# Idle products on TensorE between attention and the first expert of a mixture of experts

## The chip, the cores and the metric

The kernel runs on one core of a Trainium2 chip. The metric is the device time of one execution in microseconds (us). Engines are named as in the profile: PE (matrix products), DVE (vector), ACT (scalar), POOL (GpSimd) and SP (which issues most of the DMAs).

## The reference, cut to what matters

Linear attention with a feature map, followed by a mixture of experts whose routing picks tokens by their logits in falling order, with a capacity of 576 tokens for each of 8 experts.

```python
def _attn_ref(q, k, v, w_phi):            # (8, 8, 576, 64)
    def phi(x):
        proj = np.einsum('bhsd,df->bhsf', x, w_phi)
        proj = proj - np.max(np.abs(proj), axis=-1, keepdims=True)
        return np.concatenate([np.exp(proj), np.exp(-proj)], axis=-1)
    q_p, k_p = (phi(q), phi(k))
    kv = np.einsum('bhsf,bhsd->bhfd', k_p, v)
    z = np.sum(k_p, axis=2)
    num = np.einsum('bhsf,bhfd->bhsd', q_p, kv)
    den = np.einsum('bhsf,bhf->bhs', q_p, z)[..., None] + 1e-06
    return num / den

def _moe_ref(x, w_gate, w1, w2):          # x (4608, 512), w1 (8, 512, 1024)
    cap = N // E
    flat = (x @ w_gate).flatten()
    for idx in np.argsort(-flat):
        tok, e = idx // E, idx % E
        if assigned[tok] >= 0 or counts[e] >= cap:
            continue
        assigned[tok] = e
        counts[e] += 1
    for e in range(E):
        mask = assigned == e
        out[mask] = np.maximum(x[mask] @ w1[e], 0.0) @ w2[e]
```

## The kernel before

The work comes in three parts, one behind the other on PE.

**Attention** (to about 321 us in the profile) runs over 16 units of two batches and two heads. Each unit transposes its rows (L130), projects them (L158), forms kv and z (L196, L201, L242) and last the numerators (`num`, L285), which DVE divides (L301). The order of all these steps is made by a planner (`Plan`): it holds a list of steps with an engine, a duration and a due time, and steps of PE take one of four PSUM tiles (`D0` to `D3`) as a slot. The last two `num` end PE's part of attention. The gate's logits come out of the same products, and DVE sums them into `L`.

**The routing of the first expert** (`routing(0)` in `moe`, about 321 to 348 us) is not planned. It is written out in order. It does not take tokens one by one: it finds the logit that is the 576th by a search over the digits of the best logit of each token, six digits of 5 or 6 bits. A round works on one digit:

- DVE compares all tokens with all values of the digit (`cmp`, L520; for the first digit L472), in several chunks;
- PE counts for each value and expert how many tokens reach it: 36 products, one for each 128 tokens, whose weights are the comparisons, 32 or 64 columns wide, and which stream the 8 columns of the experts (L530). The first digit was counted in part during attention; only 9 products are left for it (L473);
- DVE turns the counts into flags (`fl`, L545 or L546);
- PE sums the flags over the digit's values by one product with ones (L548, the flag product);
- DVE takes the largest sum (L550) and moves the tokens' keys by it (L554).

After the sixth round DVE knows the expert (`ei`, L568; SP reads it and starts the loads of `w1`) and the tokens that belong to it. Two products (L582, L583) add up how many such tokens stand ahead of each row, the offsets. DVE and POOL then build two one-hot matrices (`lo` at L606, `hv` at L600), 18 products (L611) turn them into the list of tokens, and four more (L618) lay it out as the index `idx`.

Tiles of this part that PE writes lie in PSUM: `rps` with two buffers, and `h0` to `h3` and `y0`, `y1`, with one buffer each. With one buffer, a new tile under the same name may be written only when all that used the last one is done.

**The feed-forward** runs over the eight experts, again in a planner's order; the later experts' routing is spread among it. Ahead of it stands a loop of 36 products of ones with ones, of 128 columns each, whose results nobody reads (L831 to L833; `warm` is 36). Then, for the first expert, POOL gathers the tokens' rows by indirect DMA (L738), PE transposes them (L743), ACT and DVE split them (L744, L745), and the products with `w1` (L767) and `w2` (L796) follow. For each product three are run, with high and low parts. All the other experts' products follow on the same queue.

At the head of the kernel seven products of a tile of zeros (`w`, named `warm`) with 512 columns each are issued in the same manner (L102 to L104).

Of the kernel before, what the change touches and what calls it, by code (L numbers as in the profile page):

```python
# [7 lines left out]
F32 = mybir.dt.float32  # L8
# [82 lines left out]
def attention(ctx, tc, nc, q, k, v, w_phi, w_gate, xs, L, C, xp, cfg={}, after=None, later=None, count=None, init=iter(())):  # L91

    B,H,S,D=q.shape
# [4 lines left out]
    ps=ctx.enter_context(tc.tile_pool(name='aps',bufs=1,space=PS))  # L98
    ident=C['ident']
    V,A,G,PE=nc.vector,nc.scalar,nc.gpsimd,nc.tensor  # L100

    w=sb.tile([128,512],BF,name='warm',bufs=1); V.memset(w,0.0)  # L102
    p=ps.tile([128,2,512],F32,name='D0',bufs=1)
# [20 lines left out]
    P=Plan(d['stay']*1e3); P.swc,P.swA,P.swO,P.wp=90.,85.,35.,d['wp']  # L124
    ND_=4
# [193 lines left out]
    for i in range(40):  # L319
        def some(x,n=1 if i<39 else 99):  # L320
            for _ in range(n):
                if next(init,0): break
        P.add(('init',i),'DVE',300.,d['init']+i*d['pitch'],some,[('init',i-1)] if i else [],lat=95.,after=1e3*(d['init']+i*d['pitch']))
    out=P.order()
    if cfg.get('show'): 
        for x in out: print(round(x['start']),round(x['end']),x['eng'],x['mode'],x['name'])
# [155 lines left out]
def moe(ctx, tc, nc, L, xs, w1, w2, out, C, MC, R0, cfg={}):  # L482
# [3 lines left out]
    V,G,A,PE=nc.vector,nc.gpsimd,nc.scalar,nc.tensor  # L486
    rp=ctx.enter_context(tc.tile_pool(name='rt',bufs=1))
    fp=ctx.enter_context(tc.tile_pool(name='ffn',bufs=2))
    ps=ctx.enter_context(tc.tile_pool(name='fps',bufs=1,space=PS))
# [6 lines left out]
    T={}  # L496
    S=lambda shape,name,dt=F32,b=1: rp.tile(shape,dt,name=name,bufs=b)
    def rps(shape): return ps.tile(shape,F32,name='rps',bufs=cfg.get('rps',2))
    WC=tuple(cfg.get('wc',(1,2,3,3)))
    def routing(r):  # L500

# [2 lines left out]
        if not last:  # L504
            R=R0 if r==0 else state()
            if r: yield from prep(R,0,NT)
            dg,OH=R['dg'],R['OH']
            c=dg[:,0]; lat=cfg.get('lat0',1.2)
            for i,(sh,bits) in enumerate(DIG):
                K=KW[i]; n=128//K; fin=i==ND-1  # L510
                part='n0' in R and i==0
                if part:
                    p=rps([K,8])
                    count0(R,p,NT//9-1)
                else:
                    cmp=S([128,NT//n,K,n],f'cmp{K}',BF,b=2)
                    cv=c.rearrange('p (g i) -> p g i',i=n)
                    g=0
                    for ck in (WC if wide else (9,))*(1 if K==32 else 2):
                        V.tensor_tensor(cmp[:,g:g+ck],cv[:,g:g+ck,None,:].to_broadcast([128,ck,K,n]),  # L520
                                        kt[i].rearrange('p (k i) -> p k i',i=n)[:,None].to_broadcast([128,ck,K,n]),op=OP.is_ge); g+=ck
                if 'rest' in R and i:
                    with tc.issue_after(R['last']):
                        for _ in R.pop('rest'): pass
                yield
                if part: pass
                elif wide:
                    p=rps([K,8])
                    for t in range(NT):
                        PE.matmul(p,cmp[:,t//n,:,t%n],OH[:,t,:],start=t==0,stop=t==NT-1)  # L530
                else:
                    p=rps([128,n,8])
                    for g in range(NT//n):
                        PE.matmul(p,cmp[:,g].rearrange('p k i -> p (k i)'),OH[:,g*n:g*n+n,:],start=g==0,stop=g==NT//n-1)  # L534
                    yield
                    mm=S([128,n,8],f'mm{n}'); V.tensor_mul(mm,p,msk[n])
                    dd=S([128,8,1],'dd',F32R)
                    with nc.allow_low_precision(reason='whole numbers under 2**13'): V.tensor_reduce(dd,mm.rearrange('p i e -> p e i'),axis=AX.X,op=OP.add)
                    yield

                    p=rps([128,8]); PE.matmul(p,Q[n],dd[:,:,0],start=True,stop=True)  # L541
                    yield
                KR=K if wide else 128
                fl=S([KR,8],f'fl{KR}',BF)
                if part: V.scalar_tensor_tensor(fl,p,-float(cap),R['n0'],op0=OP.add,op1=OP.is_ge)  # L545
                else: V.tensor_scalar(fl,p,float(cap),2.0**(-7*i),op0=OP.is_ge,op1=OP.mult)  # L546
                yield
                p=rps([128,8]); PE.matmul(p,ones[0:KR],fl,start=True,stop=True)  # L548
                if r: yield
                ch=S([128,1],'ch'); V.tensor_reduce(ch,p,axis=AX.X,op=OP.max)  # L550
                lat=cfg.get('latd',.7)
                if fin: break
                c2=S([128,NT],'cc',BF,b=2)
                V.scalar_tensor_tensor(c2,c,ch,dg[:,i+1],op0=OP.subtract,op1=OP.add); c=c2  # L554
                if r: yield

            f8=S([128,8],'f8')
            V.scalar_tensor_tensor(f8,p,ch,e8,op0=OP.is_equal,op1=OP.mult)
            c1=S([128,1],'c1'); V.tensor_scalar(c1,ch,-2.0**(-7*(ND-1)),None,op0=OP.add)
            mx=S([128,1],'mx'); V.tensor_reduce(mx,f8,axis=AX.X,op=OP.max)  # L560
        else:
            f8=S([128,8],'f8'); V.tensor_mul(f8,opn,e8)
            mx=S([128,1],'mx'); V.tensor_reduce(mx,f8,axis=AX.X,op=OP.max)
# [17 lines left out]
        p=rps([128,2])  # L581
        PE.matmul(p,tri,tot,start=True,stop=False)  # L582
        PE.matmul(p[:,1:2],low,tot[:,0:1],start=False,stop=True)  # L583
        if r: yield
        off=S([128,2],'off'); V.tensor_copy(off,p)
        rk=S([128,2,NT],'rk')
        for i in range(2):
# [21 lines left out]
        p=rps([128,9,2,2])  # L609
# [4 lines left out]
        if wide:  # L614

            pb=S([128,9,2,2],'pb',BF); V.tensor_copy(pb,p)
            p=rps([128,9])
# [4 lines left out]
        else:  # L622
# [6 lines left out]
            p=rps([128,9,2])  # L629
# [20 lines left out]
    ctx.enter_context(tc.manual_schedule())  # L650

    it0=routing(0)
    for x in it0:
        if x=='ei':
# [12 lines left out]
    P=Plan(d['stay']*1e3); P.SEM=d['sem']; P.wp=d['wp']  # L667
# [21 lines left out]
    for r in range(1,E):  # L689
        it=routing(r)  # L690
        z=steps(r==E-1)
        t=d['TE']*(r-1)+(d['ch'] if r>1 else d['c1'])
        ni=len(z)-(2 if r<E-1 else 1)
        for i,x in enumerate(z):
            def f(y,it=it): next(it,None)
            nm=('idx',r) if i==ni else ('up',r) if i>ni else ('rt',r,i)
            if len(x)>2 and x[2]=='ei':

                nm=('ei',r)
            sl=(('idx',3,('idx',r)),) if i==ni else ()  # L700
            add(nm,x[0],float(x[1]),t+i*d['cp' if r>1 else 'cp1'],f,(prev,),mode=x[2] if x[0]=='PE' else None,slot=sl,lock=x[0]=='DVE')
            prev=nm
# [136 lines left out]
@with_exitstack  # L839
def tile_kernel(ctx, tc, q, k, v, w_phi, moe_w_gate, moe_w1, moe_w2, out):  # L840
    nc = tc.nc
    dp = ctx.enter_context(tc.tile_pool(name='dram', bufs=1, space=bass.MemoryType.DRAM))
    xs = dp.tile([4608, 512], F32, name='xs')
    lp = ctx.enter_context(tc.tile_pool(name='lp', bufs=1))
    L = lp.tile([128, 36, 8], F32, name='L')
    C = consts(ctx, tc, nc, w_phi)
    xp = ctx.enter_context(tc.tile_pool(name='xp', bufs=2))
    rp = ctx.enter_context(tc.tile_pool(name='mc', bufs=1))
    MC, R0 = [], {}

    def init():
        yield from moe_consts(rp, nc, C, L, MC, {'lat0': 2.95, 'latr': 2.33, 'latc': 1.56, 'slack': 0.66, 'slack1': -0.2, 'pre': 0, 'warm': 36, 'wide': 1, 'latd': 0.46, 'lq': 0.96, 'lo': 0.49, 'lm': 1.69, 'lat7': 3.76, 'lgh': 1.56, 'lgx': 1.29, 'xs': 13, 'xb': 3, 'c0': 1, 'x0': 7, 'w0v': 1, 'xn': 4, 'w2o': 22, 'hc': 272, 'r1d': 1.56, 'w2s': 10, 'r1s': 0.0})
        R0.update(MC[0]())

    def prep(bp):
        yield from MC[1](R0, 9 * bp, 9 * bp + 9)

    def after():
        it = prep(3)
        for _ in range(6):  # L860
            next(it)
        R0['rest'] = it

    with ExitStack() as actx:
        attention(actx, tc, nc, q, k, v, w_phi, moe_w_gate, xs, L, C, xp, ATT, after, prep, lambda bp, p: MC[2][1](R0, p, bp), init())
    moe(ctx, tc, nc, L, xs, moe_w1, moe_w2, out, C, MC, R0, {'lat0': 2.95, 'latr': 2.33, 'latc': 1.56, 'slack': 0.66, 'slack1': -0.2, 'pre': 0, 'warm': 36, 'wide': 1, 'latd': 0.46, 'lq': 0.96, 'lo': 0.49, 'lm': 1.69, 'lat7': 3.76, 'lgh': 1.56, 'lgx': 1.29, 'xs': 13, 'xb': 3, 'c0': 1, 'x0': 7, 'w0v': 1, 'xn': 4, 'w2o': 22, 'hc': 272, 'r1d': 1.56, 'w2s': 10, 'r1s': 0.0})
# [27 lines left out]
```

## Time and profile before

| | |
|---|---|
| runs | 821.05, 822.28, 822.49 us (median 822.28) |
| the profiled execution | 824.51 us |
| its span, first to last instruction | 822.7 us |
| mean granted PE clock | 0.968 |
| PE busy | 775.6 us (94%), 9932 products |
| DVE busy | 561.9 us (68%) |
| ACT, POOL busy | 363.1 us (44%), 262.3 us (32%) |

The page gives busy times of each engine, the span in 40 slices, the DMA queues, the chain that ended last and the costliest groups. The timeline lists instructions with their start and length and, in brackets, the idle time before them with what ended it. The busy time by windows gives, for stretches that the reader chooses, the length, then for PE, PE's weight loads, DVE, ACT and POOL the busy time and the count, then the granted PE clock as a share of full speed, the DMA engines' busy share and their GB/s. Times count from the span's start. A product's length in the timeline includes its way through the array, so that products overlap.

### The profile page before, as it was taken

What the parts mean: (1) busy time and instruction counts of PE and PEld (TensorE: products, weight loads), DVE (VectorE), ACT (ScalarE), POOL (GpSimd) and SP (SyncE); (2) the same over time, 40 slices, a digit from 0 to 9 for tenths busy, and PEclk for the clock granted to TensorE, in tenths of its full rate; (3) what the DMA queues carried; (4) which work ended last, traced back from release to release, by engine and by line L of the source; (5) the groups of instructions that cost most, each with busy time, mean ns of one, the idle gap of its engine ahead of it and who ended that gap; (6) DMA issues with size and microseconds to landing.
All of it is one profiled execution on the core that took longest, in us unless ns stands there. A gap on an engine that the chain in (4) does not pass through costs nothing.

```text
span 822.7 us, 23414 instructions
## 1 busy us (share of the span) xinstructions
PE 775.6 (94%) x9932; PEld 671.2 (82%) x9932; DVE 561.9 (68%) x1494; ACT 363.1 (44%) x625; POOL 262.3 (32%) x300
## 2 busy tenths in 40 slices
PE   6889999998999897589999999999999999999995
PEld 5778878887888786579889898798798898897983
DVE  4897897889788775788587577577586686460410
ACT  3656666776666562134342333243243234341410
POOL 2866655555566451120310411302203103402011
PEclk7999999999999899589999999999999999999998
DMA  9744454544554112231633333325315315700300
GB/s 193 159 118 119 120 144 114 149 120 117 149 144 118 31 32 60 88 108 69 199 122 98 102 123 118 96 108 162 110 50 180 141 50 163 269 1 39 122 26 32
DMA packets 73528, 91.79 MB, mean 112 GB/s; under 512 B 5280, under 2 KB 56512, under 8 KB 73424
## 3 DMA queue, kind: packets, MB, share of 16 engines
q1 hardware_dynamic: 67328, 71.32, 29.4%
q0 software_dynamic: 6096, 18.98, 6.7%
q8 instruction: 78, 1.28, 0.7%
q14 instruction: 26, 0.21, 0.1%
HBM read 71.40 MB, written 18.87 MB: 110 GB/s over the span
## 4 chain that ended last, share of the span: by engine, by line
PE 43%; issue 16%; POOL 2%; DMA 0%; POOLq 0%; ACT 0%; ACTq 0%
PE h L767 20%; PE y L796 17%; PE y L811 2%; PE h L743 2%; PE rps L534 1%; POOL out_dram L825 1%; POOL xg L738 1%; DMA xg<-xs,idx 0%; PE rps L611 0%; POOLq L889 0%; PE rps L541 0%; POOL spacer L824 0%; PE rps L548 0%; ACT ysb L819 0%; ACT xh L744 0%
## 5 line engine op out<-in xcount | busy, mean ns | idle before, releaser
L767 PE MATMUL h<-xh,w1h 128*128 128x272 f32 (+1 forms) x512 | 145.7, 305 | 0.7 <-ACT xh L744 0.7
L767 PE MATMUL h<-xh,w1l 128*128 128x304 f32 (+1 forms) x512 | 143.7, 300 | 0.0
L778 ACT ACTIVATE fh<-h 128x272 fp32r<-128x272 f32 (+1 forms) x128 | 49.3, 385 | 134.4 <-PE h L767 116.5
L825 POOL DMA_INDIRECT out_dram<-ysb,idx x40 | 40.7, 1016 | 206.5 <-ACT ysb L819 203.1
L796 PE MATMUL y<-w2h,fl 128*128 128x512 f32 x256 | 102.0, 398 | 0.0
L796 PE MATMUL y<-w2l,fh 128*128 128x512 f32 x256 | 101.9, 398 | 0.0
L796 PE MATMUL y<-w2h,fh 128*128 128x512 f32 x256 | 101.4, 396 | 0.0
L767 PEld LDWEIGHTS h<-xh,w1h 128*128 128x128 f32 x512 | 97.1, 190 | 2.5 <-issue 1.2
L767 PEld LDWEIGHTS h<-xh,w1l 128*128 128x128 f32 x512 | 97.2, 190 | 0.0
L738 POOL DMA_INDIRECT xg<-xs,idx x40 | 39.9, 997 | 178.5 <-issue 141.8
L767 PE MATMUL h<-xl,w1h 128*128 128x272 f32 (+1 forms) x512 | 91.6, 298 | 0.0
L782 DVE SCALAR_TENSOR_TENSOR fl<-h,fh 128x272 fp32r<-128x272 f32 (+1 forms) x128 | 52.9, 420 | 55.3 <-ACT fh L778 34.9
L268 ACT ACTIVATE qP<-D 128x768 f32<-128x768 f32 x96 | 72.4, 809 | 39.9 <-PE D L130 39.9
L209 POOL TENSOR_TENSOR ks<-ks,kP 128x512 f32<-128x512 f32 x64 | 81.9, 1280 | 4.7
L285 PE MATMUL D<-kz,qP 128*64 128x73 f32 x2304 | 80.3, 228 | 2.6 <-DVE kt L165 2.6
L208 POOL TENSOR_TENSOR ks<-kP 128x512 f32<-128x512 f32 x32 | 40.8, 1274 | 124.8 <-issue 96.3
L285 PEld LDWEIGHTS D<-kz,qP 128*64 128x64 f32 x2304 | 75.6, 136 | 5.2 <-DVE kt L165 2.7
L767 PEld LDWEIGHTS h<-xl,w1h 128*128 128x128 f32 x512 | 75.5, 188 | 0.0
L819 ACT COPY ysb<-y 128x512 f32<-128x512 f32 (+1 forms) x40 | 21.8, 545 | 103.7 <-PE y L796 65.7
L162 DVE TENSOR_REDUCE km<-D 128x6 f32<-128x768 f32 x48 | 45.8, 954 | 28.8 <-PE D L158 28.7
L196 PE MATMUL D<-kP,vi 128*64 128x256 f32 x512 | 61.6, 382 | 0.0
L796 PEld LDWEIGHTS y<-w2h,fh 128*128 128x128 f32 x256 | 48.2, 188 | 9.0
(176 smaller groups left out, 1495.0 us busy)
## 6 DMA issues: line engine op xcount, KB each, us to landing
raww<-in_moe_w_dram SPq DMA_DIRECT2D x64, 512.0 KB, 4.9
qi<-in_q_dram SPq DMA_DIRECT2D x32, 288.0 KB, 5.5
xs<-xp SPq DMA_DIRECT2D x16, 576.0 KB, 4.0
ki<-in_k_dram SPq DMA_DIRECT2D x32, 160.0 KB, 3.8
vi<-in_v_dram SPq DMA_DIRECT2D x32, 160.0 KB, 3.1
ki<-in_k_dram SPq DMA_DIRECT2D x32, 128.0 KB, 3.5
vi<-in_v_dram SPq DMA_DIRECT2D x32, 128.0 KB, 3.4
xg<-xs,idx POOLq DMA_INDIRECT x40
```

Source lines behind the costliest of these rows:

```text
L162: V.tensor_reduce(m[:,:,0:n],X['v'],axis=AX.X,op=OP.max,apply_absolute_value=True)
L196: PE.matmul(kv[64*c:64*c+64,i,0:256],v_[:,a,s_,:],kP[:,b,:],start=b in (0,5,9,14),stop=False,skip_group_check=True)
L208: if i==0: G.tensor_add(ks[:,:,a],X(0),X(1))
L209: elif i<3: G.tensor_add(ks[:,:,a],ks[:,:,a],X(i+1))
L268: for fh in range(2): A.activation(rows(qP[:,fh]),halves(X['T'],6),AF.Exp,scale=1.0-2*fh)
L285: PE.matmul(p[64*ab:64*ab+64,c,m:m+73],T['qP',u,jj][:,fh,o,64*ab:64*ab+64],T['kz',u][:,ab,fh,a^ab,:],start=fh==0,stop=fh==1,skip_group_che ...
L738: G.indirect_dma_start(out=T['xg',r][0:n,bb,:],out_offset=None,in_=xs,in_offset=bass.IndirectOffsetOnAxis(ap=T['idx',r][0:n,bb,:],axis=0))
L767: PE.matmul(p,ws[:,k,o:o+128],xx[:,k,o1:o2],start=n==0,stop=n==11)
L778: A.activation(hh[:,f,o1:o1+m1],p[:,0:m1],AF.Relu)
L782: V.scalar_tensor_tensor(hl[:,f,o1:o1+m1],p[:,0:m1],0.0,hh[:,f,o1:o1+m1],op0=OP.max,op1=OP.subtract)
L796: PE.matmul(p,hx[:,f,o:o+128],ws[:,f%2,:],start=n==0,stop=n==23)
L825: st=G.indirect_dma_start(out=ov,out_offset=bass.IndirectOffsetOnAxis(ap=iv,axis=0),in_=yv,in_offset=None)
```

## The change

Three loops of products are added whose results nobody reads.

- `keep`, a step of the planner in attention, behind the last `num`: 14 products of the tile of zeros with 512 columns, into one of the four `D` tiles. The planner puts it behind the last product of attention, ahead of the first count of the routing.
- `idle(9)` behind the flag product of each of the first five rounds, and `idle(24)` behind that of the sixth: products of ones with ones, 128 columns each.
- `idle(36)` behind the two products of the offsets.

`idle` opens a new tile named `h3` for every eight products. `r` is the expert; only the first one's routing (r = 0) gets them. DVE, ACT, POOL and SP have the same instructions in the same order as before. Line numbers behind the first added loop grow by 4, those behind the second by 8, and further on by 9 and 10.

```diff
@@ attention, behind the last unit
+    def keep(x):
+        p=bank(('D','keep'))(x)
+        for _ in range(14): PE.matmul(p[:,0],w[:,0:128],w,start=True,stop=True)
+    P.add('keep','PE',3000.,1e6,keep,[(('num',1),NU-1)],mode='A',slot=(('D',ND_,('D','keep')),),frees=(('D','keep'),))
     out=P.order()
@@ moe
     def rps(shape): return ps.tile(shape,F32,name='rps',bufs=cfg.get('rps',2))
+    def idle(n):
+        for i in range(n):
+            if i%8==0: p=ps.tile([128,512],F32,name='h3',bufs=1)
+            PE.matmul(p[:,0:128],ones,ones,start=True,stop=True)
@@ routing, each round
                 p=rps([128,8]); PE.matmul(p,ones[0:KR],fl,start=True,stop=True)
                 if r: yield
+                else: idle(24 if fin else 9)
                 ch=S([128,1],'ch'); V.tensor_reduce(ch,p,axis=AX.X,op=OP.max)
@@ routing, the offsets
         PE.matmul(p[:,1:2],low,tot[:,0:1],start=False,stop=True)
         if r: yield
+        else: idle(36)
         off=S([128,2],'off'); V.tensor_copy(off,p)
```

PE's order at the end of the sixth round before (`tri` and `low` are the triangular weights of the offsets, `cmp` is here the one-hot matrix `lo`):

```order
L548 LDWEIGHTS onesb
L548 MATMUL rps<-fl_6115,onesb 128x8 [waits DVE_49]
L582 LDWEIGHTS tri
L582 MATMUL rps<-tot,tri 128x2 [waits DVE_49]
L583 LDWEIGHTS low
L583 MATMUL rps<-tot,low 128x1
L611 LDWEIGHTS cmp_6174 [waits DVE_49]
L611 MATMUL rps<-hv,cmp_6174 128x36 [waits Pool_49]
```

With the change, where `idle(24)` ends and `idle(36)` begins (L506 is the product in `idle`):

```order
L506 LDWEIGHTS onesb
L506 MATMUL h_6207<-onesb 128x128
L591 LDWEIGHTS tri
L591 MATMUL rps<-tot,tri 128x2 [waits DVE_49]
L592 LDWEIGHTS low
L592 MATMUL rps<-tot,low 128x1
L506 LDWEIGHTS onesb
L506 MATMUL h_6255<-onesb 128x128 [waits PE_49]
```

The offsets' products now stand behind 24 idle ones, and the index's products behind 36 more; the first product on each new `h3` waits for PE's own earlier ones.

## The prediction

> **What bounds the kernel now.** I read the page's slices first: the busy share of PE and the clock that it was granted.
>
> ```profile
> PE   6889999998999897589999999999999999999995
> PEclk7999999999999899589999999999999999999998
> ```
>
> A slice is 20.57 us. Apart from the start PE is full except in the sixteenth to eighteenth slice (309 to 370 us), where the clock falls to 0.5 and 0.8 as well: the routing of the first expert, between attention and the feed-forward. What comes after it I read from the busy time by windows:
>
> ```profile
> 360.20:815.00 454.80, 453.14 (x3347) 395.80 (x3345) 276.42 (x833) 154.27 (x328) 78.59 (x114) 1.00 0.32 109
> ```
>
> PE (first pair of columns) works 453.14 of these 454.80 us at full clock. So whatever moves the start of the first expert moves the end by as much. The stretch itself, from PE's timeline (start, length, operation; in brackets the idle time before it and who ended it):
>
> ```profile
> 315.94 4.79 PE L285 MATMUL D<-kz,qP 128*64 128x73 f32 x144
> 324.50 0.70 PE L473 MATMUL rps<-OH,cmp 128*32 128x8 bf16 x9 [3.77 <-DVE xp L301]
> 325.60 0.16 PE L548 MATMUL rps<-fl,onesb 32*128 32x8 bf16 x1 [0.40 <-DVE fl L545]
> 326.57 1.43 PE L530 MATMUL rps<-OH,cmp 128*32 128x8 bf16 x36 [0.81 <-DVE cmp L520]
> 328.24 0.16 PE L548 MATMUL rps<-fl,onesb 32*128 32x8 bf16 x1 [0.24 <-DVE fl L546]
> 329.21 1.43 PE L530 MATMUL rps<-OH,cmp 128*32 128x8 bf16 x36 [0.81 <-DVE cmp L520]
> ...
> 334.51 2.24 PE L530 MATMUL rps<-OH,cmp 128*64 128x8 bf16 x36 [0.81 <-DVE cmp L520]
> ...
> 340.44 0.16 PE L548 MATMUL rps<-fl,onesb 64*128 64x8 bf16 x1 [0.25 <-DVE fl L546]
> 342.61 0.16 PE L582 MATMUL rps<-tot,tri 128*128 128x2 bf16 x1 [2.00 <-DVE tot L579]
> 342.63 0.17 PE L583 MATMUL rps<-tot,low 128*128 128x1 bf16 x1
> 346.06 1.25 PE L611 MATMUL rps<-hv,cmp 128*128 128x36 bf16 x18 [3.26 <-POOL hv L600]
> 347.60 0.25 PE L618 MATMUL rps<-pb,dup 128*128 128x9 bf16 x4 [0.29 <-DVE pb L616]
> 347.70 3.24 PE L833 MATMUL h<-onesb 128*128 128x128 bf16 x36
> 352.85 0.63 PE L743 MATMUL h<-ident,xg 128*128 128x128 f32 x4 [1.91 <-DMA xg<-xs,idx]
> 353.97 1.09 PE L743 MATMUL h<-ident,xg 128*128 128x128 f32 x4 [0.49 <-DMA xg<-xs,idx]
> 355.22 1.09 PE L743 MATMUL h<-ident,xg 128*128 128x128 f32 x4 [0.17 <-DMA xg<-xs,idx]
> 356.98 0.59 PE L767 MATMUL h<-xh,w1h 128*128 128x272 f32 x1 [0.67 <-ACT xh L744]
> ```
>
> It is one chain: DVE compares, PE counts (L473, L530), DVE makes a flag, PE sums it (L548), six times over; then the offsets (L582, L583), the index (L611, L618), the gather, the transposes (L743) and the first real product (L767). PE waits in the gaps that the change fills.
>
> **When the clock falls and rises.** Windows of 1 us place the steps (the number behind the last bracket is the granted clock):
>
> ```profile
> 326.00:327.00 1.00, 0.43 (x11) 0.43 (x12) 0.96 (x5) 0.00 (x0) 0.00 (x0) 0.54 1.15 349
> 349.00:350.00 1.00, 1.00 (x13) 1.00 (x11) 0.96 (x4) 0.24 (x1) 0.69 (x2) 0.52 1.06 372
> 353.00:354.00 1.00, 0.51 (x5) 0.30 (x4) 0.00 (x0) 0.48 (x2) 0.77 (x1) 0.69 0.74 172
> 360.00:361.00 1.00, 1.00 (x16) 0.91 (x15) 1.00 (x3) 0.00 (x0) 0.00 (x0) 0.90 0.00 0
> ```
>
> A mean of 0.54 between 1.0 and 0.5 means a fall at 326.08; likewise a rise at 349.96, a fall at 353.38, a rise at 360.20. The distances are 23.88, 3.42 and 6.82 us: seven, one and two times 3.41. So the clock is decided every 3.41 us, from what PE did in between. What counts there? Six such windows:
>
> ```profile
> 268.05:271.46 3.41, 1.70 (x28) 1.18 (x26) 3.41 (x10) 1.06 (x2) 2.08 (x3) 1.00 0.00 0
> 278.29:281.70 3.41, 3.18 (x75) 2.95 (x71) 1.48 (x9) 2.50 (x4) 1.50 (x2) 1.00 0.02 5
> 319.25:322.66 3.41, 1.48 (x48) 1.33 (x42) 3.20 (x17) 0.00 (x0) 0.00 (x0) 1.00 0.03 7
> ...
> 329.49:332.91 3.42, 2.37 (x63) 2.22 (x63) 1.95 (x9) 0.00 (x0) 0.00 (x0) 0.50 0.00 0
> ...
> 346.56:349.97 3.41, 3.02 (x38) 2.82 (x39) 2.47 (x12) 2.09 (x2) 1.16 (x2) 0.50 0.97 330
> 349.97:353.38 3.41, 1.50 (x21) 1.22 (x18) 1.99 (x7) 1.04 (x1) 2.80 (x3) 1.00 0.76 224
> ```
>
> After the first two and the last one the clock falls, after 319.25 it stays, after 346.56 it rises, after 329.49 it stays low although PE looks busy for 2.37 us. Busy time does not decide it (3.18 us fell, 1.48 us stayed). The columns that are streamed do. First their price. L833's 36 products of 128 columns ran 2.26 us at half clock, then, but for a tail of some 0.17, 0.81 us at full: (2.26/2 + 0.81)/36 = 0.054 us each at full clock, 0.107 at half. By columns the window at 319.25, 1.48 us of L285 less the tail, streams 1.3 us, **38%**, and holds. The one at 349.97 has 0.81 us of L833 and four L743 of about (0.63 - 0.17)/4 = 0.115 us: 1.27 us at most, **37%** (less if transposes count less), and falls. The L530 windows stream 8 columns a product, a few per cent, and never rise. The rise came with 22 x 0.107 = 2.35 us of L833 and about 0.3 of L611, **78%**.
>
> **The change part by part.** All of it is PE's work, and nothing else is moved on PE or on any other engine.
>
> *keep*: 14 products of 512 columns, 14 x 4 x 0.054 = 3.0 us, from 320.73 to 323.8. The gap before L473 lasts to 324.50: hidden. It fills the window to 322.66, and the next has 1.1 us of it and 0.45 of the first idle(9): 45%, so that on this grid the fall moves from 326.08 to 329.49.
>
> *What a high clock is worth in a round*: at the low one 36 loads and products take 1.43 us (L530). L473, at clock 1.00, takes 0.70 for nine, no less per product, so the gain is bounded by nothing below and by half of 1.43 above; and DVE sets a floor:
>
> ```profile
> 328.04 0.15 DVE L546 TENSOR_SCALAR fl<-rps 32x8 bf16<-32x8 f32 x1 [0.25 <-PE rps L530]
> ...
> 328.94 0.97 DVE L520 TENSOR_TENSOR cmp<-cc,kt 128x128 bf16<-128x128 bf16 x4
> ...
> 334.23 1.84 DVE L520 TENSOR_TENSOR cmp<-cc,kt 128x128 bf16<-128x128 bf16 x8
> ```
>
> The last of four compares ends at 329.91, and 12 products at half price follow: PE would end at 330.3 instead of 330.64. So 0 to 0.3 us a round; likewise 0 to 0.3 with 64 columns. One more round at full clock: I take **-0.1**.
>
> *idle(9)*: at full clock 9 x 0.054 = 0.49 us in a gap of 0.81. But the ninth product opens a new buffer of the one-buffer tile h3 and waits for the eighth. No row shows a PE product waiting for its direct predecessor; the bounds are nothing, and a product's tail (0.16 for an 8-column product, 0.21 at half clock by the two steps above) plus a wake of 0.05 (L546 ends at 328.19, L548 starts at 328.24): 0.26. I take 0.26. Still hidden at full clock. At half clock: 9 x 0.107 + 0.26 = 1.22 us against 0.97 from L548 to L530 (328.24 to 329.21): L530 is 0.25 late. Three rounds pay this. The first tiles of a round wait for DVE's short compares anyway, which swallows half: **+0.4** (0 to +0.75).
>
> *Does idle(9) hold the clock?* A round lasts 2.64 us (328.24 to 330.88): 0.49/2.64 = 18%; two bursts in one window make 0.97/3.41 = 28%. Both are under the 37% after which it fell.
>
> The Trainium skill's page "TensorE: Matmul & The Clock Gate" ("Why this matters for your kernels") says otherwise: the clock stays up as long as PE has no gap over about 3 us between bursts, and with idle(9) no gap is that long. This trace does not bear that out: the window at 278.29 was 3.18 us busy out of 3.41 and the clock fell.
>
> *idle(24)*: at half clock 24 x 0.107 + 2 x 0.26 = 3.09 us, against 2.17 from L548 to L582: **+0.9** (+0.4 if the waits cost nothing, 0 if the clock is up).
>
> *idle(36)*: at half clock 36 x 0.107 + 4 x 0.26 = 4.9 us against 3.43 from L583 to L611. L611's 18 products also wait for DVE inside, 1.25 us for some 0.55 of work, which gives 0.7 back. And with both blocks PE streams about 77% of the time, as in the window that rose, so the clock should come up on the way (on this grid at 346.56); the rest then costs half. **+0.1** (0 to +0.8).
>
> *L833* ends a microsecond later or earlier; behind it lies the gather's 1.91 us of waiting: nothing.
>
> *The clock at the first expert.* L767 ran 3.2 us at half clock before the rise at 360.20. If it starts 1.3 us later on the same grid, the window to 360.20 is only half full, and the rise waits for 363.6: 5.3 us at half, (5.3 - 3.2)/2 = +1.05. On another grid it is as much the other way. I take **+0.2** (-1.0 to +1.1).
>
> Here is the same on the pieces of PE's order. Round two before (fl is the flag, cmp the comparisons of the next round):
>
> ```order
> L530 MATMUL rps<-OH,cmp_5915 32x8
> L548 LDWEIGHTS onesb
> L548 MATMUL rps<-fl_5957,onesb 128x8 [waits DVE_49]
> L530 LDWEIGHTS cmp_5965 [waits DVE_49]
> L530 MATMUL rps<-OH,cmp_5965 32x8
> ```
>
> With the change, the end of idle(9) in the same round (L506 is idle's product, L538 the old L530):
>
> ```order
> L506 LDWEIGHTS onesb
> L506 MATMUL h_5998<-onesb 128x128
> L506 LDWEIGHTS onesb
> L506 MATMUL h_6007<-onesb 128x128 [waits PE_49]
> L538 LDWEIGHTS cmp_6013 [waits DVE_49]
> L538 MATMUL rps<-OH,cmp_6013 32x8
> ```
>
> The load of cmp now stands behind a product that waits for PE itself. DVE, which waits only for the flag product, isn't touched.
>
> **Sum:** -0.1 + 0.4 + 0.9 + 0.1 + 0.2 = **+1.5 us**. Against the profiled execution that is 822.7 + 1.5 = 824.2 us of span (824.5 + 1.5 = 826.0 with what lies around it). The median of the three runs, 822.28, is 2.2 us below that execution's time; the difference carries over: **823.8 us**.
>
> **The rivals.**
>
> *The clock holds throughout* (idle(9) suffices). For it: only two of the falls lie close to the limit, and what counts is my inference. Then all idle blocks are hidden (24 x 0.054 + 2 x 0.22 = 1.74 against 2.17; 36 x 0.054 + 4 x 0.22 = 2.8 against 3.43), five rounds gain 0 to 0.3, L611 nothing, and half of it is lost again as L767 starts earlier at half clock: -0.3 to -2.5, about -1.2: 821.1 us. This is where the skill's rule leads. Chance 18%.
>
> *The waits on PE itself cost nothing* while the clock falls: idle(9) ends where L530 starts (0.96 against 0.97), idle(24) costs 0.4, idle(36) 0.4 less L611's slack: +0.4: 822.7 us. 20%.
>
> *The clock comes up late* (the slower side): at 77% the window may just miss what it needs; L582's wait in between takes some of it. Then idle(36) runs at half clock to its end and pushes L611 by 0.8 more, and L767 begins 2 us later, with its own late rise: +1.5 + 0.8 + 0.6 = +2.9: 825.2 us. It decides as soon as the share needed is over some 75%. 12%.
>
> *The forecast* (clock falls one window later, waits cost, a rise by idle(36)): 50%.
>
> **How the numbers follow.** Runs of this kernel can be told apart by about 0.2%, 1.64 us (the three before lie 1.4 us apart). The forecast is just inside; with the clock's grid moving it by a microsecond either way, 45% of it is slower by more. Slower: 0.5 x 0.45 + 0.12 x 0.9 + 0.02 = 0.35. Faster: 0.18 x 0.4 + some from the others, 0.07 = 0.14. The rest, 0.51, is within 0.2%. The range takes in the holding clock's middle and the late rise: 820.8 to 825.6.
>
> **What would show it.** Right: the granted clock at 1.0 to about 329.5 and at 0.5 by the fourth round; L538 some 0.1 to 0.25 us late in the rounds at 0.5; the first product of the offsets 2.9 to 3.2 us behind the last flag product; the index products 1 to 1.5 us later than 347.60. Wrong: a clock of 1.0 from 320 to 346; no gap before the ninth idle product; the offsets still 2.17 us behind the last flag product.

## The result and the profile after

The changed kernel is slower: median 826.87 us (826.03 to 828.79, 6 runs) against 822.44 us (821.05 to 824.23, 6 runs), ratio 1.0056 with an interval of 1.004 to 1.0072. Two repetitions (below) gave the changed kernel the same median, 826.76 and 826.86 us, but the kernel before 824.64 and 824.63 us over 34 and 35 runs: ratios 1.0025 (1.001 to 1.0041) and 1.0018 (1.0001 to 1.0034). So the change costs some 2 us (2.1 and 2.2 by the medians, 2.1 and 1.5 by the ratios). The six runs of before in the first measurement were low by about as much, and why stays open. One execution of before at 1499 us and one of e6 at 967 us belong to a far slower state and stand in no median here.

The slices of the changed kernel's page, PE's busy share and its granted clock:

```profile
PE   6899999998999899979999999999999999999995
PEclk9999999999999899589999999999999999999998
```

The page of before had PE at 7, 5 and 8 tenths in the sixteenth to eighteenth slice; now it has 9, 9 and 7. PE is busier and the clock in the seventeenth slice is again 0.5. Windows of 1 us of the changed kernel (granted clock third from the end) place its steps:

```profile
329.00:330.00 1.00, 0.94 (x20) 0.69 (x19) 0.96 (x4) 0.00 (x0) 0.00 (x0) 0.84 0.00 0
...
346.00:347.00 1.00, 0.94 (x11) 0.78 (x9) 0.93 (x4) 0.00 (x0) 0.21 (x1) 0.63 1.09 344
356.00:357.00 1.00, 0.51 (x5) 0.30 (x4) 0.47 (x3) 0.58 (x2) 1.00 (x1) 0.99 0.70 148
363.00:364.00 1.00, 1.00 (x7) 0.88 (x8) 0.97 (x4) 0.37 (x1) 0.00 (x0) 0.59 0.00 0
```

A fall at 329.68 (before 326.08), a rise at 346.75, a fall at 356.99, a rise at 363.81. PE's timeline of the changed kernel (L326 is keep, L506 idle, L538 the count, L556 the flag product, L591 and L592 the offsets, L621 and L628 the index, L777 the first real product):

```profile
320.75 3.20 PE L326 MATMUL D<-warm 128*128 128x512 bf16 x13
324.60 0.70 PE L477 MATMUL rps<-OH,cmp 128*32 128x8 bf16 x9 [0.65 <-DVE xp L301]
...
326.67 1.43 PE L538 MATMUL rps<-OH,cmp 128*32 128x8 bf16 x36
...
330.99 0.16 PE L556 MATMUL rps<-fl,onesb 32*128 32x8 bf16 x1 [0.24 <-DVE fl L554]
331.08 1.35 PE L506 MATMUL h<-onesb 128*128 128x128 bf16 x9
332.36 1.36 PE L538 MATMUL rps<-OH,cmp 128*32 128x8 bf16 x36
333.97 0.16 PE L556 MATMUL rps<-fl,onesb 32*128 32x8 bf16 x1 [0.24 <-DVE fl L554]
...
341.39 0.16 PE L556 MATMUL rps<-fl,onesb 64*128 64x8 bf16 x1 [0.25 <-DVE fl L554]
341.48 3.17 PE L506 MATMUL h<-onesb 128*128 128x128 bf16 x24
344.45 0.21 PE L591 MATMUL rps<-tot,tri 128*128 128x2 bf16 x1
344.52 0.16 PE L592 MATMUL rps<-tot,low 128*128 128x1 bf16 x1
344.71 3.84 PE L506 MATMUL h<-onesb 128*128 128x128 bf16 x36
348.39 0.77 PE L621 MATMUL rps<-hv,cmp 128*128 128x36 bf16 x18
349.44 0.25 PE L628 MATMUL rps<-pb,dup 128*128 128x9 bf16 x4 [0.29 <-DVE pb L626]
```

Attention ends 0.09 us later than in the first profile. Against that, the flag products of the first three rounds stand where they stood; the fourth comes 0.33 us later, the fifth 0.59, the sixth 0.85, the offsets 1.76, the index (349.44 against 347.60) 1.76. The idle time before L538 is gone, and with it the slack.

To compare kernels whose attention ends at different times, I cut each span at the start of the last num, of the last flag product, of the index product and of the first L767. All are starts in PE's timeline, in us:

| profile | to last num | to sixth flag | to index | to first L767 | to the end | last num to end |
|---|---|---|---|---|---|---|
| before | 320.50 | 19.94 | 7.15 | 9.39 | 465.73 | 402.2 |
| before, again (c1) | 320.76 | 19.93 | 7.15 | 9.82 | 466.17 | 403.1 |
| changed | 320.59 | 20.79 | 8.06 | 9.31 | 466.31 | 404.5 |
| changed, again (a1) | 320.10 | 21.13 | 8.06 | 9.32 | 466.36 | 404.9 |
| changed, third (a2) | 320.27 | 20.79 | 8.06 | 9.25 | 466.10 | 404.2 |
| keep alone (e1) | 318.26 | 19.94 | 7.15 | 9.10 | 467.86 | 404.0 |
| no waits (e2) | 318.55 | 20.29 | 7.63 | 9.16 | 465.97 | 403.1 |
| idle(9) alone (e3) | 321.18 | 21.46 | 7.14 | 9.43 | 468.06 | 406.1 |
| the last two blocks (e4) | 319.68 | 19.93 | 8.06 | 9.19 | 466.34 | 403.5 |

From the last num to the end the three profiles with the change average 404.5, the two before 402.65: 1.9 us, close to the repeated timings. Attention's own stretch, the same work in all nine, lies between 318.3 and 321.2 (321.6 in e6 and 317.3 in e9 below). That spread is larger than the effect.

### The profile page after: what moved, and what is told of

The parts are those of the page before. It is cut to its first block, busy times and chain, and to the rows that moved or that the text cites. A ratio compares the mean times of both kernels' runs of the same rounds, so it can differ in the third digit from the quotient of the medians.

```text
span 825.1 us, 23651 instructions
## 1 busy us (share of the span) xinstructions
PE 789.1 (96%) x10050; PEld 679.9 (82%) x10051; DVE 562.1 (68%) x1494; ACT 363.1 (44%) x625; POOL 262.4 (32%) x300
## 4 chain that ended last, share of the span: by engine, by line
PE 45%; issue 12%; POOL 2%; DMA 0%; DVE 0%; POOLq 0%; ACT 0%; DVEq 0%; ACTq 0%
PE h L777 20%; PE y L806 16%; PE y L821 2%; PE h L753 2%; PE rps L542 1%; POOL out_dram L835 1%; PE h L506 1%; PE rps L538 1%; POOL xg L748 1%; DMA xg<-xs,idx 0%; PE rps L621 0%; PE rps L556 0%; POOLq L899 0%; PE rps L549 0%; POOL spacer L834 0%
## 5 line engine op out<-in xcount | busy, mean ns | idle before, releaser
L777 PE MATMUL h<-xh,w1h 128*128 128x272 f32 (+1 forms) x512 | 146.1, 305 | 0.7 <-ACT xh L754 0.7
L777 PE MATMUL h<-xh,w1l 128*128 128x304 f32 (+1 forms) x512 | 143.9, 301 | 0.0
L777 PEld LDWEIGHTS h<-xh,w1h 128*128 128x128 f32 x512 | 97.3, 190 | 2.5 <-issue 1.2
L777 PEld LDWEIGHTS h<-xh,w1l 128*128 128x128 f32 x512 | 97.5, 190 | 0.0
L777 PE MATMUL h<-xl,w1h 128*128 128x272 f32 (+1 forms) x512 | 91.4, 298 | 0.0
L777 PEld LDWEIGHTS h<-xl,w1h 128*128 128x128 f32 x512 | 75.5, 188 | 0.0
```

Source lines behind the costliest of these rows:

```text
L777: PE.matmul(p,ws[:,k,o:o+128],xx[:,k,o1:o2],start=n==0,stop=n==11)
```

## The experiments

The diffs are cut to the changed lines and, where needed, one line beside them.

**c1: the kernel before, once more** (no edit).

> The kernel before, unchanged, once more, for a second profile and for the spread of its runs. In the two profiles the index products (L618) start 1.84 us later with the change and the last product ends 2.35 us later, yet the medians lie 4.4 us apart. Theory A (delay plus a later rise of the clock; the rest is the spread of executions, in which the first profile of before was a slow one): this profile has the same stretch to within 0.2 us (last L285 to L618: 26.9 us), some 2 to 5 us of L767 at half clock depending on where the clock's steps fall, and a span between 819 and 823 us. Theory B (the kernel before usually has the clock up when L767 starts, and the first profile was an exception): under 1 us of L767 at half clock and a span near 820.6 us.

824.61 us, ratio to before 1.0002 (0.9989 to 1.0016). The stretches are those of the first profile to within 0.5 us, with L767 at half clock for 3.0 us. Theory A, but for the span: 823.8 us where 819 to 823 were expected, and the first profile of before, at 822.7 us, was the shorter of the two, so that this part of the theory failed. The 35 runs of before beside it ran from 821.48 to 826.99.

**a1 and a2: the full change, again and a third time** (no edit).

> The full change once more. In the four profiles so far a span is the sum of three stretches: attention to its last num (318.3 to 320.8 us, other from run to run by where the clock falls in it, in kernels whose attention is the same), from there to the first L767 (36.5 and 36.9 us before, 38.2 with the change), and from there to the end (465.7 to 467.9). Theory A (the change's own cost is the middle stretch, +1.3 to +1.7 us, and a later rise of the clock, 0 to +1; the 4.4 us of the first measurement hold 2 us of the executions' spread): 1.3 to 3 us over the kernel before, whose median is now 824.24 over 35 runs: 825.5 to 827.2. Theory B (the cost really is 4.4 us): over 828.

> The full change a third time, since the first measurement gave +4.4 us (6 runs of each) and the second +2.1 (12 and 34 runs). In the profiles, from the last num to the end, it took 404.5 and 404.9 us, the kernel before 402.2 and 403.1. Theory A (its own cost is about 2 us; the rest of the first measurement was the spread of executions): +1.2 to +3.0 us. Theory B (4.4 us is real): +3.5 or more.

+2.1 and +2.2 us by the medians. Theory A both times. In a1 the clock fell at 326.2, a step earlier than in the first profile of the change, so that one round more ran its block at half clock: the sixth flag product comes 1.19 us later instead of 0.85. Where the step falls differs from execution to execution.

**e1: keep alone.**

```diff
-                else: idle(24 if fin else 9)
-        else: idle(36)
```

> Only the 14 products behind the last num are left; the three kinds of idle are taken out. Theory A: they lie in PE's gap, the clock falls one step of 3.41 us later, L530 takes 1.43 us at full clock too, so nothing is gained or lost: within 0.7 us of before (822.4). Rival (the later fall is worth something, or the block itself does harm later on): more than 1 us away from before.

825.23 us, ratio 1.0009 (0.9991 to 1.0027). The time by itself cannot tell; the stretches can: sixth flag product and index are as before to 0.01 us, so keep costs and wins nothing there. The odd number is the last one, 467.86 us, taken up under e5.

**e2: no waits inside a block.**

```diff
-            if i%8==0: p=ps.tile([128,512],F32,name='h3',bufs=1)
+            if i==0: p=ps.tile([128,512],F32,name='h3',bufs=1)
```

> The whole change, but each idle block writes one tile instead of a new h3 for every eight products, so that no product in a block waits for its predecessor. Theory A (the waits on PE itself are a large part): rounds at half clock 0 to 0.1 us late instead of 0.3 each, the offsets 0.4 to 0.6 us behind instead of 0.9, L618 starts 0.5 us late instead of 1.74, and the time is 1 to 2 us under that of the full change: 825 to 826 us. Rival (the cost is in the products at half clock, not in the waits): within 0.7 us of the full change (826.9).

825.23 us, ratio 1.0010 (0.9992 to 1.0028). The index comes 0.83 us late, more than the 0.5 expected. Four of e2's rounds ran at half clock, and so a1 is the one to compare with, which also had four: there the index comes 2.10 us late. The waits are 1.3 us of that, some 60%, and the products at half clock the rest. A round of e2 at half clock, from PE's timeline:

```profile
329.07 0.16 PE L556 MATMUL rps<-fl,onesb 32*128 32x8 bf16 x1 [0.24 <-DVE fl L554]
329.17 1.14 PE L506 MATMUL h<-onesb 128*128 128x128 bf16 x9
330.24 1.35 PE L538 MATMUL rps<-OH,cmp 128*32 128x8 bf16 x36
```

From flag product to count 1.17 us, where before had 0.97 and the full change has 1.37.

**e3: idle(9) alone.** The planner's step keep is taken out too.

```diff
-                else: idle(24 if fin else 9)
+                elif not fin: idle(9)
-        else: idle(36)
```

> Only idle(9) behind the first five flag products is left. Theory A: without the first block the clock falls a step earlier, so that four of the five rounds run it at half clock, each 0.26 to 0.33 us late: sixth flag product 1.1 to 1.3 us later (21.1 us behind the last num, 19.94 before), time 1.0 to 1.5 us over before. Rival (idle(9) streams enough to hold the clock once it is alone): sixth flag product at 19.9, clock 1.0 to its end.

826.13 us, ratio 1.0027 (1.0011 to 1.0044). The clock falls at 323.9 and all five rounds are late, one more than expected, by 0.33 three times and 0.26 twice: 1.52 us at the sixth flag product. Idle(9) by itself does not hold the clock, and alone it costs more than idle(24) and idle(36) do in e4. Within the full change, with three or four rounds at half clock, it costs 0.85 to 1.19 us, about as much as idle(24).

**e4: idle(24) and idle(36) alone.** keep is taken out too.

```diff
-                else: idle(24 if fin else 9)
+                elif fin: idle(24)
```

> Only idle(24) behind the sixth flag product and idle(36) behind the offsets are left. Theory A: the clock is down when they start; the offsets come 0.9 us later, the index 0.9 to 1.7 us later (later if the clock does not rise on the way), time 823.5 to 825 us. Theory B (the loss is in where the rise of the clock falls for the first expert): as far from before as the full change, 826 to 827 us.

824.19 us, ratio 1.0005 (0.9988 to 1.0023). The offsets come 0.90 us later, the index 0.91: all of it idle(24)'s, and idle(36) adds nothing, though it runs 3.84 us as in the full change: L621 (here L620) begins 0.49 us later behind the offsets (3.94 against 3.45) and is shorter by the same (0.77 against 1.25). The time shows less than the 0.9 of the profile, within its interval.

**e5: hold the clock from the index to the first L767** (the kernel before, with idle products elsewhere).

```diff
-    for i in range(cfg.get('warm',0)):
+    for i in range(64):
                 for k in range(4): PE.transpose(...)
+                if r==0 and bb<3:
+                    z=ps.tile([128,512],F32,name='y1',bufs=1)
+                    for _ in range(10): PE.matmul(z[:,0:128],ones,ones,start=True,stop=True)
```

> The kernel before with idle products at another place: 64 instead of 36 ahead of the feed-forward, and 10 behind each of the first three groups of transposes of the first expert (L743), so that PE streams between the index and the first L767. Theory A (a share of some 38% of streamed columns in 3.41 us holds the clock, and the loss worth winning is L767 at half clock, 3 us at half speed): the clock stays at 1.0 from about 350 us, L743 takes 0.63 us in every group, no L767 at half clock, and from the last num to the end 1.5 to 2.2 us less than before. Rival (the clock falls anyway, or the products delay the transposes): within 0.7 us, or slower.

826.21 us, ratio 1.0026 (1.0002 to 1.0049): slower, and theory A fell, though the clock did what it said. It was at 1.0 when L767 (here L770) began. But then, in PE's timeline of e5:

```profile
358.29 0.29 PE L770 MATMUL h<-xh,w1l 128*128 128x272 f32 x1
360.25 0.39 PE L534 MATMUL rps<-OH,cmp 128*128 128x32 bf16 x9 [1.67 <-DVE cmp L520]
```

PE is out of work 1.67 us before the second expert's first count, which stands next in its queue and needs DVE's comparisons. And DVE has no gap there; its timeline in e5:

```profile
355.76 0.69 DVE L748 TENSOR_TENSOR xl<-h,xh 128x512 fp32r<-128x512 f32 x1 [0.17 <-ACT xh L747]
...
358.48 0.68 DVE L726 TENSOR_TENSOR w1l<-raww,w1h 128x512 fp32r<-128x512 f32 x1
359.08 0.45 DVE L464 TENSOR_TENSOR OH<-scb,sm 128x288 bf16<-128x288 bf16 x1
359.45 0.75 DVE L520 TENSOR_TENSOR cmp<-dg,kt 128x1152 bf16<-128x1152 bf16 x1
```

At half clock, as in the profile of before, the same count begins without a wait:

```profile
360.50 0.39 PE L534 MATMUL rps<-OH,cmp 128*128 128x32 bf16 x9
```

From the index to this count it takes 12.6 to 13.5 us in the profiles in which L767 began at half clock and 12.9 to 13.7 in those in which it began at full clock. So the first 4 us of L767 are bound by DVE: a full clock there only makes PE wait. The wait then lets the clock fall for 3.4 us of dense work, in e5's windows:

```profile
358.58:362.00 3.42, 1.54 (x19) 1.23 (x18) 3.39 (x8) 0.37 (x1) 0.00 (x0) 1.00 0.00 0
362.00:365.40 3.40, 3.40 (x17) 3.28 (x16) 3.02 (x9) 0.79 (x2) 0.00 (x0) 0.51 0.02 5
```

From the count to the end e5, e1, e3 and e8 (below), which began L767 at full clock, need 464.1 us, the others 462.2 to 462.6; from L767 to the end that is 467.9 to 468.1 against 465.7 to 466.4.

**e6: hold the clock through the routing.**

```diff
-            if i%8==0: p=...
+            if i==0: p=...
+                if wide: idle(8)
                 KR=K if wide else 128
-                else: idle(24 if fin else 9)
+                else: idle(36 if fin else 18 if K==64 else 16)
-        else: idle(36)
+        else: idle(50)
```

> The full change with more products and no waits: one tile for each block, 8 products behind each count, 16 (18 with 64 columns) behind each flag product, 36 behind the sixth, 50 behind the offsets: 41 to 49% of each round streams. Theory A: the clock stays at 1.0 from attention to the index, and this wins nothing in the rounds, since L530 took 1.43 us at full clock too: sixth flag product at 19.8 to 20.2 us behind the last num, index within 0.4 us of before, time within 1 us of before. Rival (a held clock shortens the rounds with 64 columns by up to 0.3 us each and the index by more): index 0.5 to 1.2 us earlier than before.

825.87 us, ratio 1.0012 (0.9997 to 1.0027). The clock stayed at 1.0 from 212 us to 355. The sixth flag product came 20.91 us behind the last num, the index 28.03, 0.94 later than before: the expectation missed by that. A round with 32 columns takes 0.30 us longer (2.95 against 2.65). The count starts 0.13 us later behind its longer block (1.10 against 0.97), and the flag product 0.18 later behind the start of the count (1.85 against 1.67), as the 8 products behind the count make it wait. In these rounds the count takes as long as at half clock (in the changed kernel's timeline above, 1.43 us at 326.67 at full clock). With 64 columns a held clock does help; e6's count of the sixth round in PE's timeline

```profile
340.31 1.73 PE L538 MATMUL rps<-OH,cmp 128*64 128x8 bf16 x36
```

and the window over it (the granted clock is third from the end):

```profile
340.31:342.04 1.73, 1.73 (x39) 1.63 (x38) 1.32 (x6) 0.00 (x0) 0.00 (x0) 1.00 0.00 0
```

1.73 us at clock 1.00 (1.84 in the fifth round), 2.23 at 0.50 before. Behind the sixth flag product nothing is won (7.11 us to the index against 7.15). So two such counts are what a held clock could win in the routing, 0.9 us by these numbers; no version tried had that gain without the blocks that hold the clock.

**e7: blocks that fit the gaps at full clock**, and **e9: the same without the loop of 36**.

```diff
-            if i%8==0: p=...
+            if i==0: p=...
+                if wide: idle(4)
                 KR=K if wide else 128
-                else: idle(24 if fin else 9)
+                else: idle(30 if fin else 16)
-        else: idle(36)
+        else: idle(40)
```

and in e9 also

```diff
-    for i in range(cfg.get('warm',0)):
+    for i in range(0):
```

> The idea of the change with counts that fit the gaps: one tile a block (no waits), 4 products behind each count, 16 behind each flag product, 30 behind the sixth, 40 behind the offsets; 36 to 45% of each round streams. Theory A (the clock is held, and a held clock shortens only the rounds with 64 columns, whose L530 took 1.73 us at full clock against 2.23): rounds with 32 columns within 0.1 us of before, the two with 64 columns 0.35 to 0.5 us shorter each, sixth flag product 19.0 to 19.3 us behind the last num (19.94 before), index 0.7 to 1.0 us earlier than before; time 0 to 1.5 us under before. Rival (the share is too small somewhere and the clock falls): the blocks then cost 0.7 us a round at half clock, index later than before.

> e7 and e8 together: blocks that fit, and no 36 products ahead of the feed-forward. Theory A: index 0.7 to 1.0 us earlier than before, L767 begins at half clock, the rest 465.7 to 466.4 us; 0.5 to 1.5 us under before. Rival: the gain of the index is lost in the transposes and the gather, within 0.5 us of before or slower.

828.31 us, ratio 1.0039 (1.0023 to 1.0054), and 827.43 us, 1.0039 (1.002 to 1.0058). The rival, both times: the clock fell at 332.9 and 332.5, and then in e7's timeline

```profile
333.98 1.88 PE L506 MATMUL h<-onesb 128*128 128x128 bf16 x16
335.78 2.08 PE L538 MATMUL rps<-OH,cmp 128*64 128x8 bf16 x36
```

16 products at half clock take 1.88 us in a gap of 0.97, so that a round costs up to 1.05 us more (0.7 was expected); e7's index comes 30.74 us behind the last num, e9's 29.66. Blocks cut to the gap at full clock are the costlier the sooner it falls. In e9 L767 began at half clock and the rest took 466.2 us, as expected.

**e8: the kernel before without the loop of 36.**

```diff
-    for i in range(cfg.get('warm',0)):
+    for i in range(0):
```

> The kernel before without the 36 products ahead of the feed-forward (the loop at L831). In the profiles in which L767 began at full clock (36.2 to 38.0 us behind the last num), PE then waited 1.6 us for DVE's comparisons, the clock fell and the rest took 467.9 to 468.1 us; where L767 began at half clock the rest took 465.7 to 466.4. Theory A (the bound there is DVE, so a low clock at L767's start costs nothing, and a clock that is up and falls again costs 1.7): without the loop L767 always begins at half clock, the rest takes 465.7 to 466.4, L743 costs at most 0.5 more; time within 1 us of before. Rival (the loop is worth what it looks like): 1.5 us or more slower than before.

824.82 us, ratio 1.0007 (0.9993 to 1.002). The time is as theory A said, its reason is not: the clock did rise before L767, on the transposes alone. A window of e8 just before L767, at half clock throughout,

```profile
351.76:355.18 3.42, 3.06 (x12) 2.29 (x12) 1.27 (x4) 1.97 (x4) 1.95 (x3) 0.50 0.60 179
```

holds nothing of PE's but these transposes, by its timeline:

```profile
352.06 3.06 PE L743 MATMUL h<-ident,xg 128*128 128x128 f32 x12 [5.23 <-DMA xg<-xs,idx]
```

Behind it the clock was 1.0, PE waited for DVE as in e5, and the rest took 468.04 us.

No version tried is clearly faster than the kernel before.

## Why the prediction was wrong, step by step

**The base of the forecast was the step that failed most.** The working forecast +1.5 us and put it on the median of three runs, 822.28, with the words that the distance to the profiled execution "carries over". Span to span it was close: 825.1 against 824.2. But the kernel before has a median of 824.2 to 824.6 over 34 or 35 runs at a time. Of the 3.1 us between 823.8 and 826.87 some 2.3 are thus the base; the rest is the change, some 2 us and not 1.5. Three runs 1.4 us apart were read as a spread of 1.4; it is over 5. The range, which should have held that, was built from the unknown costs alone and ended 1.3 us under the first median, 826.87. Why those first runs of before were all low isn't settled. The profiles show attention's stretch between 317.3 and 321.6 us with clock falls at other places in each, but none of the first timed runs left a trace. Nor is the spread alone a good reason: of the 104 later runs of before 44 lie at or under 824.23, the highest of the first six, and six out of six would then come up in under 1% of draws. So it can't be excluded that in the first measurement the change did cost more than 2 us.

**The rounds: +0.4 forecast, 0.85 and 1.19 measured.** The mechanism was right, two sizes were not. First, L538 begins not 0.25 but 0.40 us late. The block's first product starts 0.09 us behind the flag product (331.08 against 330.99), which the sum left out. Here are the ninth idle product and the count behind it in the changed kernel:

```profile
332.17 0.27 PE L506 MATMUL h<-onesb 128*128 128x128 bf16 x1
332.36 0.19 PE L538 MATMUL rps<-OH,cmp 128*32 128x8 bf16 x1
```

Eight products at 0.107 from 331.08 would end at 331.94, and the ninth starts at 332.17, as the wait's price of 0.26 said to within 0.03. But the count then began 0.19 us behind the ninth product instead of 0.107, which no term had either. Second, "swallows half" was wrong: the count got shorter by 0.07 us with 32 columns (1.43 to 1.36) and 0.15 with 64 (2.23 to 2.08), about a sixth and a third. I had taken the swallowed part without working it out from DVE's compares.

**idle(24): +0.9 forecast, 0.90 measured.** **idle(36): +0.1 forecast, 0.0 measured**, with the rise on the way at 346.75, forecast for 346.56. **keep: nothing**, as forecast, e1 shows it. **The clock falls one step later**: 329.68, forecast 329.49. That is in part the luck of the grid: in a1, with the same products, it fell at 326.22, 6.1 us behind the last num instead of 9.1. **Idle(9) doesn't hold the clock**: shown by the profile of the change and by e3. So the rival is refuted to which the rule of the Trainium skill's page "TensorE: Matmul & The Clock Gate" ("Why this matters for your kernels") led, no gap over some 3 us: with the change PE's longest gap from 320.75 to the fall at 329.68 is the 0.65 us before L477, and the clock fell.

**A round's gain from a high clock: -0.1 forecast, nothing measured**: the counts with 32 columns take 1.43 us at either clock. The gain that exists, 0.5 us in a count with 64 columns, lay where the clock was down, and is more than the 0.3 that the prediction allowed.

**The clock at the first expert: +0.2 forecast with 1 us either way.** L777 ran 5.06 us at half clock, as worked out for this grid (5.3). But its price was wrong: from L767 to the end the change took 466.1 to 466.4 us, before 465.7 and 466.2, some 0.3 more and not 1.05. e5 shows why: DVE bounds the first 4 us there, so that part of the lost speed is hidden. The prediction had called the whole stretch PE's, from a window that begins at 360.2, behind the place in question.

Together: 0.85 to 1.2 for the rounds, 0.9 for idle(24), nothing for idle(36), and the last two stretches, index to L767 and L767 to the end, cancel: about 1.9 us, against 1.5 forecast and 2.1 and 2.2 by the repeated medians. The sum came this close because 0.3 too much for idle(36) and the first expert made up for part of the rounds. The sign for the index, 1 to 1.5 us late, was missed with them: 1.76.

## What to carry to other kernels

Before filling gaps to hold PE's clock, work out the share that the filling streams in one of the clock's windows, at both clocks: a block that fits its gap at full clock and is too thin to hold it is paid at half clock, at twice its length. Ask first what the clock is worth there: small counts on 32 columns, and a stretch that another engine bounds, win nothing. And take the base of a forecast from as many runs as its effect needs; three runs 1.4 us apart say nothing about a spread of five.

## What the runs showed of the hardware

The clock's rule came out sharper than expected. For each of the 14 profiles of this study I summed PE's streamed columns in each of the 3.41 us windows (0.053 us for 128 columns at full clock, 0.107 at half, twice that for fp32 products outside the feed-forward's, and weighted by the share of the array's rows and columns that the product used). From 15 us on, with 81 falls and 78 rises, no window that streamed more than 38% was followed by a fall, and none under 36% kept the clock; no rise came under 72%, and no window over 74% stayed low. Both weights are needed: without the array's share a window of 97% was followed by a fall, and with fp32 counted once one of 18% kept the clock. Weight loads and the way through the array are not in this sum and weren't needed. Transposes count: behind e8's window with twelve of them and nothing else on PE, the clock rose. The Trainium skill's page "TensorE: Matmul & The Clock Gate" (Part 4: PE-mode transpose) says that the full clock does not engage for them; behind e8's window it did.

A weight load of 32 columns with its 8-column product starts every 33 ns at either clock in the rounds' counts (before and e6); one of 64 columns starts every 53 ns at half clock and every 32 at full, where DVE's chunks do not hold it up.

A product that waits for the one before it on PE started 0.37 us behind it at half clock (0.26 over the usual 0.107), and the next load behind such a block came 0.09 us later than a product would have (0.14 in e2, whose block has no wait).
